# Query sums, two more key tiles and the keys' high part: three transfers in place of engine work, in a fused attention and two-layer kernel

## The chip, the cores and the metric

The kernel runs on one core of one Trainium2 chip. A core has five engines that run side by side: TensorE (PE, with its weight loads as PEld), VectorE (DVE), ScalarE (ACT), GpSimd (POOL) and SyncE (SP, which here only issues transfers). Each works through its own instructions in the order in which the program puts them. The metric is the time of one execution on the device in microseconds; less is better. Before the change the median of three runs is 679.89 us (678.85 to 679.95).

## The reference

```python
q_pool = q.reshape(B, H, S // 2, 2, D).mean(axis=3)     # B 2, H 8, S 1152, D 64
scores = scale * (q_pool @ k.T)                         # 576 pooled queries, 1152 keys
attn = exp(scores - max) / (sum + 1e-9)
x = (attn @ v), heads side by side                      # 1152 tokens, 512 wide
h = x @ w_in1                                           # 512 to 2048
x = where(h >= 1, h, where(h <= -1, 0, (h + 1)**2 / 4)) @ w_out1
h = x @ w_in2
out = (h * sigmoid(h)) @ w_out2
```

Inputs q, k, v are float32; the weights are float64.

## The kernel before

Matrix products are made exact enough by parts: every operand is split into a high part, rounded to the type float32r, and a low part, the difference. The product of two operands is then two or three products of parts. `ident` and `ident_r` are the identity in float32 and in float32r.

Attention runs head by head, 16 of them. For a head, keys, queries and values are loaded with 128 rows on partitions. **Keys**: ACT copies the loaded tile `kraw` into half 0 of `khl`, rounding it (`hi`, line 446); POOL writes the low part into half 1 (`lo_of`, line 138); PE turns the nine pieces, high and low stacked (line 464), and ACT or DVE moves them to `kk`. **Queries**: POOL adds the two rows of a pair into half 0 of `qs` (line 481); SP copies half 0 to half 1 by a transfer (`twice`, line 488); PE turns the four pieces of `qs` with the float32 identity `ident` (line 496); ACT and DVE make the parts `qm`. **Scores** (line 570): PE multiplies a row tile of 128 queries with the 1152 keys in three banks; DVE moves each bank, negated, to a tile `p` and keeps the row minimum (line 577); ACT takes the exponential in place (line 590). There are eight `p` tiles, so two heads' worth. **Values**: the probabilities have to be turned, nine key tiles of 128 by 512 per head. For key tiles 0 to 3 PE turns the four pieces straight from the `p` tiles with `ident` (line 630). For key tiles 4 to 8 SP first copies the columns from `p` to a float32r tile `pr` (line 597; one tile `pr0` for key tiles 4 and 5, one `pr1` for 6 to 8, list `COPIED`), and PE turns them from there with `ident_r` (line 634). ACT moves a turned tile out of its bank and DVE (`KINDS` "psum": lines 608, 609) or POOL ("pool": lines 614, 138) makes the parts `thl`, and PE multiplies them with the value parts (line 647). Queries 512 to 575 of two heads share one row tile, `pt` (lines 676, 685). Behind the attention run the two layers (lines 158, 203, 205).

What order the instructions stand in is settled when the program is built. Every step is an `op` with a due time, the engine with an assumed occupancy and latency, the steps that it needs, and the buffers that it holds (`Buf`, counted in `room`). `plan_out` walks through them with these assumed numbers and gives each engine its list; the rows of order below are its outcome. On the chip each engine follows its list and waits for what is not there yet.

Of the kernel before, what the change touches and what calls it, by code (L numbers as in the profile page):

```python
# [8 lines left out]
F32 = mybir.dt.float32  # L9
# [9 lines left out]
def fused_kernel(  # L19
# [11 lines left out]
    nc = tc.nc  # L31
# [22 lines left out]
    WARM = 7  # L54
    COPIED = ((4, 2), (6, 3))
    AHEAD = 3.0
# [287 lines left out]
    with ExitStack() as at, ExitStack() as keys, ExitStack() as prep:  # L344
# [15 lines left out]
        khls = several(nat, 2, [P, KC, 2, D], F32R, "khl")  # L360
        qss = several(nat, 2, [P, NM, 2, D], F32, "qs")
        kks = several(qk, 3, [P, KC, P], F32R, "kk")
        qms = [several(qk, 2, [P, NM * P], F32R, f"qm{i}") for i in range(2)]
        qts = [several(qk, 2, [P, 3, QT], F32R, f"qt{i}") for i in range(2)]
        ps_ = several(pp, 2 * NM, [P, S], F32, "p")
        pts = several(pp, 1, [P, S], F32, "pt")
# [8 lines left out]
        tiny = fixed.tile([P, 1], F32, name="tiny")  # L375
        room.update(qraw=2, kraw=2, vraw=1, khl=2, qs=2, kk=3, qm=2, qt=2, qtraw=2, qts=1, p=2 * NM, pt=1, **{f"pr{i}": 1 for i in range(len(COPIED))}, thl=THL, pf=PF, vhl=2)
        room.update(y2=2, rb=2, z=1, b=6, y=2, w=1)
# [31 lines left out]
        def inputs(h):  # L409
# [34 lines left out]
            for part in [slice(3 * g, 3 * g + 3) for g in range(3)] if h == 0 else [slice(0, KC)] * 1:  # L444
                n = (part.stop - part.start) / KC
                hi = lambda part=part: nc.scalar.copy(khls[kb.slot][:, part, 0], kraws[kr.slot][:, part])
                khi.append(op(t1, ("ACT", 0.08 + 0.5 * n, 0.17 + 0.51 * n, hi), [lk], [kr, kb]))
                lo = lambda e, part=part: lambda: lo_of(e, khls[kb.slot][:, part, 1], kraws[kr.slot][:, part], khls[kb.slot][:, part, 0])
                ways = [("POOL", 0.2 + 1.175 * n, 0.25 + 1.18 * n, lo(nc.gpsimd))]
                if not h:  # L450
                    ways.insert(0, ("DVE", 0.1 + 0.6 * n, 0.18 + 0.6 * n, lo(nc.vector)))
                klo.append(op(t1 + 0.01, ways, [khi[-1]], [kr, kb], both=not h))
            if h:
# [20 lines left out]

            qb, bank, mb = Buf("qs"), Buf("b"), Buf("qm")
            qm[h] = mb

            def split_q(e):
                t = qraws[qr.slot]
                if h:  # L480
                    e.tensor_add(qss[qb.slot][:, :, 0], t[:, :, 0], t[:, :, 1])
                else:
                    e.tensor_add(qss[qb.slot], *(t[:, :, r].unsqueeze(2).to_broadcast([P, NM, 2, D]) for r in range(2)))

            t3 = base(h - 2) - 0.1 * PERIOD
            if h:
                sq = op(t3, ("POOL", 0.7, 0.76, lambda: split_q(nc.gpsimd)), [lq], [qr, qb])
                twice = lambda: nc.sync.dma_start(out=qss[qb.slot][:, :, 1], in_=qss[qb.slot][:, :, 0])
                sq = op(t3 + 1, ("SP", 0.5, 2.6, twice), [sq], [qb])
            else:  # L490
# [3 lines left out]
            def turn_q():  # L494
                for i in range(NM):
                    nc.tensor.transpose(banks[bank.slot][:, i * P : (i + 1) * P], qss[qb.slot][:, i].rearrange("p a d -> p (a d)"), ident)  # L496

            o = op(t4, ("PE", 0.436, 0.6, turn_q), [sq], [qb, bank])
            o1 = op(t4 + 0.5, ("ACT", 0.483, 0.62, lambda: nc.scalar.mul(qms[mb.slot][0], banks[bank.slot], SCALE)), [o], [bank, mb])

# [117 lines left out]
        def values(h):  # L618
# [5 lines left out]
            for c in range(KC):  # L624
# [12 lines left out]
                if x:  # L637
                    do = lambda x=x[0], f=turn_copy: f(x=x)
                    o = op(tc_, ("PE", 0.27, 0.45, do), [o_r[h, x[0], i] for i in range(NM)], [bank, pr_of[h, x[0]]])
                else:  # L640
# [314 lines left out]
```

## Time and profile before

| | |
|---|---|
| median of three runs | 679.89 us |
| the profiled execution | 680.63 us, its span 678.5 us |
| PE busy, share of the span | 670.0 us, 99% |
| POOL, ACT, DVE busy | 438.0, 420.2, 524.0 us |
| attention, roughly | the first 280 us of the span |
| share of the 16 DMA engines, 20 to 255 us | 0.53 |

A row of the list of groups or of the view by stretches gives busy time; busy PE time contains overlap of one matmul with the next, so what a block of matmuls costs is read from when the next block starts. A row of the waits names who ended an engine's idle time. The chain of work that ended last tells which work set the end.

### The profile page before, as it was taken

Reading aid. Unit: us, or ns where it says so; the run is one execution under the profiler, and the core shown is the slowest. Engines: PE = TensorE matmul, PEld = TensorE weight load, DVE = VectorE, ACT = ScalarE, POOL = GpSimd, SP = SyncE. Lnnn points to the kernel's source line nnn. Section 1 sums busy time; section 2 is a strip of 40 time slices with the busy share of each in tenths; the row PEclk is TensorE's granted clock in tenths of the full one; section 3 lists DMA queues with packets and bytes.
Section 4 is the critical chain, followed back from the end, with each engine's and each line's share of the span. In section 5 each row is a group of like instructions: output and inputs, shape, how many; then the busy total and the mean of one; then the engine's idle time right before and its main releaser. Section 6 shows DMA issues by size and latency. Waiting matters only on the chain.

```text
span 678.5 us, 11815 instructions
## 1 busy us (share of the span) xinstructions
PE 670.0 (99%) x3962; PEld 623.5 (92%) x3962; DVE 524.0 (77%) x1180; ACT 420.2 (62%) x808; POOL 438.0 (65%) x414
## 2 busy tenths in 40 slices
PE   8999999999999999999999999999999999999997
PEld 6899988999999979999999999999999999999996
DVE  6879898988888898389898995996983794892223
ACT  5989998999898888455644443455554543442221
POOL 5788999999797878546646453486853553553221
PEclk8999999999999999999999999999999999999999
DMA  7866655645433356113333231231231331300012
GB/s 214 213 212 177 188 165 169 179 145 173 130 115 109 98 167 205 47 63 109 110 103 117 93 122 34 95 95 61 94 125 37 116 98 38 118 1 0 1 48 93
DMA packets 54988, 75.90 MB, mean 112 GB/s; under 512 B 14736, under 2 KB 40592, under 8 KB 54928
## 3 DMA queue, kind: packets, MB, share of 16 engines
q1 hardware_dynamic: 54640, 74.73, 35.3%
q8 instruction: 31, 0.51, 0.3%
q10 hardware_dynamic: 288, 0.43, 0.2%
q14 instruction: 29, 0.24, 0.1%
HBM read 49.81 MB, written 2.39 MB: 77 GB/s over the span
## 4 chain that ended last, share of the span: by engine, by line
PE 94%; DVE 2%; DMA 2%; ACT 1%; issue 1%; DVEq 0%; ACTq 0%
PE bank L158 30%; PE bank L203 15%; PE bank L205 15%; PE bank L570 12%; PE bank L647 10%; PE bank L630 4%; PE bank L634 3%; PE bank L685 3%; PE bank L464 1%; PE bank L676 1%; DMA pr<-p 1%; PE bank L496 1%; DMA qraw<-in_q_dram 1%; DVE p L577 0%; DVE part L217 0%
## 5 line engine op out<-in xcount | busy, mean ns | idle before, releaser
L138 POOL TENSOR_TENSOR gl<-gf,gh 128x384 fp32r<-128x384 f32 x96 | 110.0, 1147 | 107.3 <-ACT gh L187 104.0
L158 PE MATMUL bank<-xh,whi 128*128 128x384 f32 x384 | 129.7, 338 | 0.0
L158 PE MATMUL bank<-xh,wli 128*128 128x384 f32 x384 | 129.2, 337 | 0.0
L158 PE MATMUL bank<-xl,whi 128*128 128x384 f32 x384 | 129.2, 336 | 0.0
L577 DVE TENSOR_SCALAR_CACHE_REDUCE p<-bank 128x384 f32<-128x384 f32 x192 | 102.0, 551 | 20.7 <-PE bank L570 14.3
L647 PE MATMUL bank<-thl,vhl 128*128 128x512 f32 x288 | 113.4, 429 | 0.0
L138 POOL TENSOR_TENSOR thl<-pf,thl 128x512 fp32r<-128x512 f32 x80 | 103.7, 1298 | 4.0 <-PE bank L647 0.7
L181 DVE TENSOR_TENSOR gf<-bank,gf 128x384 f32<-128x384 f32 x96 | 52.9, 551 | 65.0 <-ACT gf L173 60.6
L570 PE MATMUL bank<-kk,qm 128*128 128x384 f32 x384 | 97.3, 357 | 0.3
L590 ACT ACTIVATE p<-p,low 128x1152 f32<-128x1152 f32 x64 | 81.5, 1274 | 2.7 <-DVE low L587 2.6
L187 ACT CAST gh<-gf 128x384 fp32r<-128x384 f32 x96 | 49.3, 513 | 49.6 <-DVE gf L181 47.6
L158 PEld LDWEIGHTS bank<-xl,whi 128*128 128x128 f32 x384 | 72.1, 188 | 4.2
L158 PEld LDWEIGHTS bank<-xh,whi 128*128 128x128 f32 x384 | 72.1, 188 | 4.0
L138 POOL TENSOR_TENSOR wli<-wf,whi 128x512 fp32r<-128x512 f32 x32 | 43.8, 1369 | 45.6 <-ACT whi L128 45.5
L570 PEld LDWEIGHTS bank<-kk,qm 128*128 128x128 f32 x384 | 66.4, 193 | 7.2 <-DVE thl L609 1.2
L158 PEld LDWEIGHTS bank<-xh,wli 128*128 128x128 f32 x384 | 72.1, 188 | 0.0
L138 POOL TENSOR_TENSOR wlo<-wf,who 128x512 fp32r<-128x512 f32 x32 | 44.0, 1374 | 37.3 <-ACT who L128 37.3
L173 ACT ACTIVATE gf<-bank 128x384 f32<-128x384 f32 x48 | 23.6, 491 | 70.8 <-PE bank L158 64.9
L116 DVE SCALAR_TENSOR_TENSOR wf<-wr,wf 128x512 uint32<-128x512 uint32 x56 | 65.0, 1160 | 1.0
L203 PE MATMUL bank<-gh,wlo 128*128 128x384 f32 x192 | 65.0, 338 | 0.0
L203 PE MATMUL bank<-gh,who 128*128 128x384 f32 x192 | 64.8, 337 | 0.0
L203 PE MATMUL bank<-gl,who 128*128 128x384 f32 x192 | 64.7, 337 | 0.0
(97 smaller groups left out, 1550.8 us busy)
## 6 DMA issues: line engine op xcount, KB each, us to landing
wr<-in_moe_w_in_dram SPq DMA_DIRECT2D x32, 512.0 KB, 3.7
wr<-in_moe_w_out_dram SPq DMA_DIRECT2D x32, 512.0 KB, 3.3
pr<-p SPq DMA_DIRECT2D x64, 192.0 KB, 2.3
pr<-p SPq DMA_DIRECT2D x64, 128.0 KB, 2.2
vraw<-in_v_dram SPq DMA_DIRECT2D x16, 288.0 KB, 3.3
kraw<-in_k_dram SPq DMA_DIRECT2D x15, 288.0 KB, 3.3
qraw<-in_q_dram SPq DMA_DIRECT2D x16, 256.0 KB, 3.4
rb<-row SPq DMA_DIRECT2D x16, 128.0 KB, 3.1
```

The source lines that it names most:

```text
L116: nc.vector.scalar_tensor_tensor(xi, st["top"], 0xC0000000, xi, ALU.bitwise_and, ALU.bitwise_or)
L138: eng.tensor_sub(out, whole, hi.bitcast(F32))
L158: nc.tensor.matmul(ps, lhsT=w[:, c, j * P : (j + 1) * P], rhs=a[:, c, ts_], start=(c == 0 and n == 0), stop=(c == ND - 1 and n == 2),)
L181: nc.vector.tensor_tensor(gf, hps.pop(i), gf, op=ALU.mult if steps[i][0] else ALU.max)
L187: nc.scalar.copy(gh, gf)
L203: nc.tensor.matmul(ps[:, :TB], lhsT=w[:, j, m * P : (m + 1) * P], rhs=a, start=start, stop=stop)
L205: nc.tensor.matmul(ps[:, cols], lhsT=a[:, m * P : (m + 1) * P], rhs=w[:, j, cols], start=start, stop=stop)
L570: nc.tensor.matmul(ps, lhsT=qq[:, c0 : c0 + P], rhs=rhs, start=n == 0, stop=n == last)
L577: nc.vector.tensor_scalar(dst, ps, -1.0, None, ALU.mult, ALU.min, accum_out=mxs[key, t][:, j : j + 1])
L590: nc.scalar.activation(pt(), pt(), AF.Exp, bias=lows[key][:, tt : tt + 1], scale=-1.0, accum_out=sums[key][:, tt : tt + 1])
L630: nc.tensor.transpose(banks[bank.slot][:, i * P : (i + 1) * P], ps_[p_of[h, i].slot][:, c * P : (c + 1) * P], ident)
L647: nc.tensor.matmul(banks[6 + yb.slot], lhsT=lhsT, rhs=thls[tb.slot][i], start=not count, stop=len(count) == 2 * KC - 1)
```

## The change

Three things are done in another way.

- Key tiles 2 and 3 are copied as well: `COPIED` has a third tile, seven of the nine key tiles are turned from copies with `ident_r`, and SP issues twelve copies for a head in place of eight. The `p` tiles become six (`STAGED`).
- The query sums stand once in `qs`, and two transfers on SP put them into both halves of a float32r tile `qd`, from which PE turns them with `ident_r`. For head 0 the sums go to the tile `y2s[0]` and are turned as before.
- For heads 3 to 15 the high part of the keys is not made by ACT. GpSimd issues a second load of the same keys from memory straight into half 0 of `khl`, with a conversion to float32r on the way. The first load stays, for the low part.

The planner's assumed cost of one turn from a copy goes from 0.27 to 0.35 us.

```diff
@@ -52,7 +52,7 @@
     PF = 2
     SLACK = 0.2
     WARM = 7
-    COPIED = ((4, 2), (6, 3))
+    STAGED, COPIED = 6, ((2, 2), (4, 2), (6, 3))
     AHEAD = 3.0
     KINDS = ("psum", "pool", "psum", "pool", "psum", "pool", "psum", "pool", "pool")
     KEVAC = [[("ACT", 0.37, 0.484), ("DVE", 0.476, 0.547)]] * 3
@@ -358,11 +358,12 @@
         kraws = several(nat, 2, [P, KC, D], F32, "kraw")
         vraws = several(nat, 1, [P, KC, D], F32, "vraw")
         khls = several(nat, 2, [P, KC, 2, D], F32R, "khl")
-        qss = several(nat, 2, [P, NM, 2, D], F32, "qs")
+        qss = several(nat, 2, [P, NM, D], F32, "qs")
+        qds = several(nat, 2, [P, NM, 2, D], F32R, "qd")
         kks = several(qk, 3, [P, KC, P], F32R, "kk")
         qms = [several(qk, 2, [P, NM * P], F32R, f"qm{i}") for i in range(2)]
         qts = [several(qk, 2, [P, 3, QT], F32R, f"qt{i}") for i in range(2)]
-        ps_ = several(pp, 2 * NM, [P, S], F32, "p")
+        ps_ = several(pp, STAGED, [P, S], F32, "p")
         pts = several(pp, 1, [P, S], F32, "pt")
 
         prs = [pp.tile([P, NM, n * P], F32R, name=f"pr{i}") for i, (_, n) in enumerate(COPIED)]
@@ -373,7 +374,7 @@
         rbs = several(pp, 2, [P, NM * P], F32, "rb")
         ztail = fixed.tile([P, P], F32, name="ztail")
         tiny = fixed.tile([P, 1], F32, name="tiny")
-        room.update(qraw=2, kraw=2, vraw=1, khl=2, qs=2, kk=3, qm=2, qt=2, qtraw=2, qts=1, p=2 * NM, pt=1, **{f"pr{i}": 1 for i in range(len(COPIED))}, thl=THL, pf=PF, vhl=2)
+        room.update(qraw=2, kraw=2, vraw=1, khl=2, qs=2, qd=2, kk=3, qm=2, qt=2, qtraw=2, qts=1, p=STAGED, pt=1, **{f"pr{i}": 1 for i in range(len(COPIED))}, thl=THL, pf=PF, vhl=2)
         room.update(y2=2, rb=2, z=1, b=6, y=2, w=1)
 
         def clear(what):
@@ -444,12 +445,16 @@
             for part in [slice(3 * g, 3 * g + 3) for g in range(3)] if h == 0 else [slice(0, KC)] * 1:
                 n = (part.stop - part.start) / KC
                 hi = lambda part=part: nc.scalar.copy(khls[kb.slot][:, part, 0], kraws[kr.slot][:, part])
-                khi.append(op(t1, ("ACT", 0.08 + 0.5 * n, 0.17 + 0.51 * n, hi), [lk], [kr, kb]))
+                if h > 2:
+                    cast = lambda: nc.gpsimd.dma_start(out=khls[kb.slot][:, :, 0], in_=k[b, hd].rearrange("(p c) d -> p c d", c=KC))
+                    khi.append(op(t0, ("POOL", 1.0, 4.5, cast), [lq, o_k[h - 2][-1]], [kb]))
+                else:
+                    khi.append(op(t1, ("ACT", 0.08 + 0.5 * n, 0.17 + 0.51 * n, hi), [lk], [kr, kb]))
                 lo = lambda e, part=part: lambda: lo_of(e, khls[kb.slot][:, part, 1], kraws[kr.slot][:, part], khls[kb.slot][:, part, 0])
                 ways = [("POOL", 0.2 + 1.175 * n, 0.25 + 1.18 * n, lo(nc.gpsimd))]
                 if not h:
                     ways.insert(0, ("DVE", 0.1 + 0.6 * n, 0.18 + 0.6 * n, lo(nc.vector)))
-                klo.append(op(t1 + 0.01, ways, [khi[-1]], [kr, kb], both=not h))
+                klo.append(op(t1 + 0.01, ways, [khi[-1], lk], [kr, kb], both=not h))
             if h:
                 khi, klo = khi * 3, klo * 3
             kb2 = kk[h] = Buf("kk")
@@ -472,30 +477,35 @@
                 ways = [(e, occ, lat, (lambda e=e, ev=evac: ev(e)())) for e, occ, lat in KEVAC[g]]
                 o_k[h].append(op(t2 + 0.5, ways, [o], [bank, kb2]))
 
-            qb, bank, mb = Buf("qs"), Buf("b"), Buf("qm")
+            qb, qb2, bank, mb = Buf("qs"), Buf("qd"), Buf("b"), Buf("qm")
+            first_q = y2s[0].rearrange("p (t a d) -> p t a d", a=2, d=D)
             qm[h] = mb
 
             def split_q(e):
                 t = qraws[qr.slot]
                 if h:
-                    e.tensor_add(qss[qb.slot][:, :, 0], t[:, :, 0], t[:, :, 1])
+                    e.tensor_add(qss[qb.slot], t[:, :, 0], t[:, :, 1])
                 else:
-                    e.tensor_add(qss[qb.slot], *(t[:, :, r].unsqueeze(2).to_broadcast([P, NM, 2, D]) for r in range(2)))
+                    e.tensor_add(first_q, *(t[:, :, r].unsqueeze(2).to_broadcast([P, NM, 2, D]) for r in range(2)))
 
             t3 = base(h - 2) - 0.1 * PERIOD
             if h:
                 sq = op(t3, ("POOL", 0.7, 0.76, lambda: split_q(nc.gpsimd)), [lq], [qr, qb])
-                twice = lambda: nc.sync.dma_start(out=qss[qb.slot][:, :, 1], in_=qss[qb.slot][:, :, 0])
-                sq = op(t3 + 1, ("SP", 0.5, 2.6, twice), [sq], [qb])
+                twice = lambda: [nc.sync.dma_start(out=qds[qb2.slot][:, :, x].bitcast(F32), in_=qss[qb.slot]) for x in range(2)]
+                sq = op(t3 + 1, ("SP", 0.9, 3.0, twice), [sq], [qb, qb2])
             else:
                 sq = op(t3, [("DVE", 0.6, 0.69, lambda: split_q(nc.vector)), ("POOL", 1.25, 1.31, lambda: split_q(nc.gpsimd))], [lq], [qr, qb], both=True)
             t4 = base(h - 2) + 0.3 * PERIOD
 
             def turn_q():
                 for i in range(NM):
-                    nc.tensor.transpose(banks[bank.slot][:, i * P : (i + 1) * P], qss[qb.slot][:, i].rearrange("p a d -> p (a d)"), ident)
-
-            o = op(t4, ("PE", 0.436, 0.6, turn_q), [sq], [qb, bank])
+                    to = banks[bank.slot][:, i * P : (i + 1) * P]
+                    if h:
+                        nc.tensor.transpose(to.bitcast(F32R), qds[qb2.slot][:, i].rearrange("p a d -> p (a d)"), ident_r)
+                    else:
+                        nc.tensor.transpose(to, first_q[:, i].rearrange("p a d -> p (a d)"), ident)
+
+            o = op(t4, ("PE", 0.35, 0.53, turn_q) if h else ("PE", 0.436, 0.6, turn_q), [sq], [qb2 if h else qb, bank])
             o1 = op(t4 + 0.5, ("ACT", 0.483, 0.62, lambda: nc.scalar.mul(qms[mb.slot][0], banks[bank.slot], SCALE)), [o], [bank, mb])
 
             def rest():
@@ -636,7 +646,7 @@
                 x = [i for i, (c0, n) in enumerate(COPIED) if c0 <= c < c0 + n]
                 if x:
                     do = lambda x=x[0], f=turn_copy: f(x=x)
-                    o = op(tc_, ("PE", 0.27, 0.45, do), [o_r[h, x[0], i] for i in range(NM)], [bank, pr_of[h, x[0]]])
+                    o = op(tc_, ("PE", 0.35, 0.53, do), [o_r[h, x[0], i] for i in range(NM)], [bank, pr_of[h, x[0]]])
                 else:
                     o = op(tc_, ("PE", 0.436, 0.6, turn), [o_p[h, i] for i in range(NM)], [bank] + [p_of[h, i] for i in range(NM)])
                 parts = split(tc_ + 0.5, bank, NM, [o], tb, KINDS[c])
```

On POOL, in the middle of the attention, before: `khl` from `kraw` is the keys' low part, L614 is the rounded copy of a turned tile, `vhl` the values' low part, `xl` the low part of a finished head pair.

```order
L138 TENSOR_TENSOR vhl_143<-vraw_105,vhl_143 128x9x64
L138 TENSOR_TENSOR thl_139<-pf_140,thl_138 128x512
L138 TENSOR_TENSOR xl<-y_145,xh 128x512
L614 CAST thl_136<-pf_141 128x512
L138 TENSOR_TENSOR khl_106<-kraw_103,khl_106 128x9x64
L138 TENSOR_TENSOR thl_137<-pf_141,thl_136 128x512
L614 CAST thl_132<-pf_140 128x512
L138 TENSOR_TENSOR vhl_143<-vraw_105,vhl_143 128x9x64
```

The same place after. L449 is the new load, L624 the rounded copy of a turned tile.

```order
L624 CAST thl_137<-pf_141 128x512
L449 DMA khl_106<-in_k_dram 128x9x64
L138 TENSOR_TENSOR thl_138<-pf_141,thl_137 128x512
L624 CAST thl_133<-pf_142 128x512
L138 TENSOR_TENSOR vhl_144<-vraw_105,vhl_144 128x9x64
L138 TENSOR_TENSOR thl_134<-pf_142,thl_133 128x512
L138 TENSOR_TENSOR khl_106<-kraw_103,khl_106 128x9x64
L624 CAST thl_139<-pf_141 128x512
```

A load is issued on POOL, and the low part of the keys that waits for its landing stands five rows behind it; both are in the row of instructions that make `thl`.

On SP, while the first two heads are under way, before: `pr` from `p` are copies, `kraw`, `qraw` and `vraw` loads for coming heads.

```order
L597 DMA pr_130<-p_122 128x256
L597 DMA pr_131<-p_122 128x384
L488 DMA qs_109<-qs_109 128x4x64
L424 DMA qraw_98<-in_q_dram 128x4x128
L597 DMA pr_130<-p_123 128x256
L597 DMA pr_131<-p_123 128x384
L420 DMA kraw_103<-in_k_dram 128x576
L597 DMA pr_130<-p_124 128x256
L597 DMA pr_131<-p_124 128x384
```

The same stretch after, up to the load of the same `kraw`:

```order
L607 DMA pr_132<-p_125 128x384
L739 DMA row<-sum 128x4
L607 DMA pr_132<-p_126 128x384
L440 DMA vraw_105<-in_v_dram 128x576
L494 DMA qd_110<-qs_109 128x4x64 x2
L742 DMA rb_147<-row 64x512
L607 DMA pr_130<-p_127 128x256
L607 DMA pr_130<-p_128 128x256
L425 DMA qraw_98<-in_q_dram 128x4x128
L607 DMA pr_130<-p_123 128x256
L421 DMA kraw_103<-in_k_dram 128x576
```

The loads for the coming heads and the doubling of the queries stand behind more copies: this load of keys was row 24 on SP and is row 36.

On PE, the first head's key tiles 2 and 3, before: both are turned from `p` right behind key tiles 0 and 1.

```order
L630 MATMUL bank_70<-ident,p_121 128x128
L630 MATMUL bank_70<-ident,p_122 128x128
L630 MATMUL bank_70<-ident,p_123 128x128
L630 MATMUL bank_70<-ident,p_124 128x128
L630 MATMUL bank_73<-ident,p_121 128x128
L630 MATMUL bank_73<-ident,p_122 128x128
L630 MATMUL bank_73<-ident,p_123 128x128
L630 MATMUL bank_73<-ident,p_124 128x128
L570 MATMUL bank_75<-kk_111,qm_115 128x384
L570 MATMUL bank_75<-kk_111,qm_116 128x384
```

After, with scores of the next head (L580) and the first product with the values (L657) ahead of them:

```order
L657 MATMUL bank_76<-thl_133,vhl_143 128x512
L580 MATMUL bank_73<-kk_113,qm_117 128x384
L580 MATMUL bank_73<-kk_113,qm_118 128x384
L580 MATMUL bank_72<-kk_113,qm_117 128x384
L580 MATMUL bank_72<-kk_113,qm_118 128x384
L644 MATMUL bank_75<-ident_r,pr_130 128x128 x4
L657 MATMUL bank_76<-thl_134,vhl_143 128x512
L657 MATMUL bank_76<-thl_135,vhl_143 128x512
L644 MATMUL bank_74<-ident_r,pr_130 128x128 x4
```

Tiles 2 and 3 of the first head are now turned from the copy `pr_130`, behind the products that stood behind them.

## Rows read from the trace of the kernel before

**Rows 1.** The page: busy times; the chain that ended last, by engine and line.

```profile
PE 670.0 (99%) x3962; PEld 623.5 (92%) x3962; DVE 524.0 (77%) x1180; ACT 420.2 (62%) x808; POOL 438.0 (65%) x414
...
PE bank L158 30%; PE bank L203 15%; PE bank L205 15%; PE bank L570 12%; PE bank L647 10%; PE bank L630 4%; PE bank L634 3%; PE bank L685 3%; PE bank L464 1%; PE bank L676 1%; DMA pr<-p 1%; PE bank L496 1%; DMA qraw<-in_q_dram 1%; DVE p L577 0%; DVE part L217 0%
```

**Rows 2.** Stretches, attention: length; busy times and counts; clock; DMA share; GB/s.

```profile
20.00:255.00 235.00, 233.24 (x1609) 211.41 (x1610) 203.59 (x662) 213.95 (x416) 205.94 (x208) 1.00 0.53 160
```

**Rows 3.** Timeline of PE, one engine: start, us, line, what, count.

```profile
126.41 0.46 PE L634 MATMUL bank<-ident_r,pr 128*128 128x128 f32 x4
126.70 0.46 PE L647 MATMUL bank<-thl,vhl 128*128 128x512 f32 x1
127.00 0.86 PE L570 MATMUL bank<-kk,qt 128*128 128x384 f32 x4
...
133.47 0.60 PE L496 MATMUL bank<-ident,qs 128*128 128x128 f32 x4
133.83 0.48 PE L647 MATMUL bank<-thl,vhl 128*128 128x512 f32 x1
134.15 0.51 PE L570 MATMUL bank<-kk,qm 128*128 128x384 f32 x2
134.50 0.60 PE L630 MATMUL bank<-ident,p 128*128 128x128 f32 x4
134.85 0.48 PE L647 MATMUL bank<-thl,vhl 128*128 128x512 f32 x1
135.17 0.37 PE L464 MATMUL bank<-ident_r,khl 128*128 128x128 f32 x3
```

**Rows 4.** Groups, whole span: the two turns of probabilities; the rounding on ACT.

```profile
L630 PE MATMUL bank<-ident,p 128*128 128x128 f32 x256 | 37.2, 273 | 0.3 <-DVE p L577 0.3
L634 PE MATMUL bank<-ident_r,pr 128*128 128x128 f32 x320 | 37.0, 239 | 0.7 <-DVE wf L120 0.6
L446 ACT CAST khl<-kraw 128x576 fp32r<-128x576 f32 x15 | 10.3, 689 | 1.9 <-POOL khl L138 1.0 <-PE bank L464 0.6 <-DMA vraw<-in_v_dram 0.3
```

**Rows 5.** Groups on POOL, 20 to 255 us: busy, mean ns, idle before and releasers.

```profile
L614 POOL CAST thl<-pf 128x512 fp32r<-128x512 f32 x72 | 44.4, 618 | 13.6 <-ACT pf L613 10.3 <-PE bank L634 3.2
L138 POOL TENSOR_TENSOR khl<-kraw,khl 128x576 fp32r<-128x576 f32 x12 | 17.3, 1442 | 0.4 <-ACT khl L446 0.2 <-PE bank L647 0.2
L481 POOL TENSOR_TENSOR qs<-qraw 128x256 f32<-128x256 f32 x12 | 8.9, 738 | 7.0 <-PE bank L496 6.4 <-DMA pr<-p 0.6
```

**Rows 6.** Timeline of SP: start, us, line, what is issued, count.

```profile
14.11 2.54 SPq L597 DMA_DIRECT2D pr<-p  x4
16.74 0.62 SPq L488 DMA_DIRECT2D qs<-qs  x1
17.41 0.66 SPq L424 DMA_DIRECT2D qraw<-in_q_dram  x1
18.16 1.16 SPq L597 DMA_DIRECT2D pr<-p  x2
19.37 0.59 SPq L420 DMA_DIRECT2D kraw<-in_k_dram  x1
```

**Rows 7.** Issues of transfers: KB of one, median us from issue to landing.

```profile
pr<-p SPq DMA_DIRECT2D x64, 128.0 KB, 2.2
kraw<-in_k_dram SPq DMA_DIRECT2D x15, 288.0 KB, 3.3
qs<-qs SPq DMA_DIRECT2D x15, 128.0 KB, 3.1
```

**Rows 8.** Stretches of ten us: the third from the start.

```profile
20.00:30.00 10.00, 10.00 (x66) 8.55 (x67) 9.32 (x32) 9.82 (x20) 7.03 (x9) 1.00 0.92 229
```

**Rows 9.** Chain of waits, 20 to 255 us: share by line; pieces (start, us, what).

```profile
by line: PE bank L570 31.2%; PE bank L647 25.2%; PE bank L630 9.8%; PE bank L634 8.9%; PE bank L685 6.4%; PE bank L464 3.3%; PE bank L676 2.9%; DMA pr<-p 2.7%; PE bank L496 2.2%; issue 1.2%; DVE p L577 1.1%; DVE thl L609 0.8%; DVE bank L108
...
80.67 2.95 DMA pr<-p
...
240.94 3.35 DMA pr<-p
```

## Prediction

> **What bounds the kernel now.** I read the page first. PE is busy for 99% of the span, and the chain that ended last lies on PE nearly throughout [rows 1]: what the change is worth is PE time saved, less the time in which PE is made to wait. The change lies in the attention, so I read one stretch of it, 20 to 255 us. There PE is busy for 233.24 of 235 us at granted clock 1.00, which is the level of 2.4 GHz; ACT is busy for 213.95 us, POOL for 205.94, DVE for 203.59 [rows 2]. PE is the bound, but three engines stand at 87% to 91%, and each feeds it. The reader should see both: every microsecond off PE counts, and little room is left to move work to the others. Third, busy PE time contains overlap, so I read the cost of a turn from the starts of blocks in the timeline [rows 3]. The groups on POOL, SP's timeline and the transfers came last, since that is where the change puts work.
>
> **Part 1: cheaper turns on PE.** A block of four turns from `p` starts at 134.50, the product behind it at 134.85 and the next block at 135.17: 0.67 us for block and product. With a block of turns from a copy the same pair runs from 126.41 to 127.00, 0.59 us [rows 3]. The difference is 0.08 us for four. Two more key tiles in 16 heads are 32 blocks: 32 x 0.08 = 2.6 us. The query turns: block and product run from 133.47 to 134.15, 0.68 us [rows 3], so a query block with `ident_r` should save 0.68 - 0.59 = 0.09, but its neighbours differ; I use 0.07 to 0.09. Fifteen heads (head 0 stays) make 1.0 to 1.4, say 1.1. The sum is 3.7 us. Another view gives the upper end: the groups' mean busy time per turn is 37.2 us / 256 = 145 ns from `p` and 37.0 / 320 = 116 ns from copies [rows 4], 29 ns apart, and 128 + 60 turns x 29 ns = 5.5 us; that busy time is modelled, so I take the starts' 3.7. Nothing hides PE's work, so these 3.7 us would all come off the time if no wait takes their place.
>
> **Part 2: ACT loses work.** Thirteen roundings of 0.689 us [rows 4] go: 9.0 us of ACT, some 8 of them within the stretch, which takes ACT from 91% to about 88%. None of it is on the chain. What it can give back is on POOL: POOL's rounded copies wait 10.3 us for ACT [rows 5].
>
> **Part 3: POOL gets thirteen loads to issue.** No row shows a transfer issued by POOL. From below: SP issues a load of the same keys in 0.59 us [rows 6]. From above: POOL's own work on the same keys takes 1.44 us [rows 5]; far above lies 3.3 us, the median from issue to landing of such a load on SP [rows 7], if POOL were held until the data are there. The issue writes addresses and moves no data, so it is nearer to the first two; between them I take 1.0 us. That is 13 us. POOL's idle time in the stretch is 235 - 205.94 = 29.1 us, less 3.7 because the stretch shortens: 25.4. Of it 10.3 are waits for ACT, which part 2 shortens, and 6.4 are sums that wait for PE to have turned the older queries out of `qs` [rows 5]; now a transfer empties `qs`, so these go. The two make 16.7 us that can be filled. At 1.0 us the loads fit, POOL rises to about (205.9 + 13) / 231.3 = 95%, and they cost nothing directly. Queued behind the load on POOL are the parts `thl` that PE's products wait for; the load itself waits for PE to have turned the keys of two heads before. The low part of the keys stands five rows behind the load. Between them the order has a rounded copy, 0.62 us, and three differences of at most 1.44 us each [rows 5], under 4.9 us; a load that lands 3.3 us [rows 7] behind its issue is there in time, one that needs over 4.9 us stops POOL.
>
> The Trainium skill (DMA: Bandwidth & Descriptors, SWDGE vs HWDGE vs iDMA) speaks against the change: the descriptors of a load issued by GpSimd are computed by code on GpSimd's own cores, where those of SP's loads come from hardware. Its section Latency and other measured facts gives about 1 us to the first byte; by that figure, as an estimate, thirteen loads take 13 us, the same sum as mine. No run here shows it yet.
>
> **Part 4: SP and the transfers.** SP issues 64 more copies at 0.58 us each (two in 1.16) and 15 more doublings at 0.62 [rows 6]: 37 + 9 = 46 us, 3 us a head, of about 15. In steady state SP has that room. Early on it has not: from 14.11 us on it issues without a gap [rows 6]. There the order puts the keys' load, at 19.37 before, twelve rows later; at 0.6 us that is 7 us, about 26.6, and with 3.3 us of landing [rows 7] the data are there at 30. The first head's tiles 2 and 3 now need a landed copy, 2.2 us [rows 7] behind its issue, where PE had turned them at once. The order puts other products in between, so I take 0.5 us of waiting here, between 0 and the 2.2 of one landing. The traffic: 64 x 128 KB, 15 x 128 KB and 13 x 288 KB are 14 MB in 235 us, 60 GB/s on top of 160 at a share of 0.53 [rows 2]; in proportion 0.73. In the third ten us the share is 0.92 already [rows 8]. Chains through a copy exist before: two pieces of 2.95 and 3.35 us, 2.7% of the stretch in all [rows 9]; under more traffic such pieces grow. PE's waits in the stretch were 235 - 233.24 = 1.8 us [rows 2]. With POOL at 95% and six `p` tiles in place of eight I let them grow by 0.7 us, bounded by 0 and by a doubling, and by a gain of the same 1.8 if ACT's relief removes them.
>
> **The sum.** -3.7 (PE) + 0.5 (early copies) + 0.7 (more waits) = -2.5 us. The profiled execution takes 680.63 us for a span of 678.5; against it the sum gives 678.1. The median of the runs is 679.89, 0.7 below the profiled one; since the sum is a difference, I set it against the median: 677.4 us.
>
> **Rivals.** *POOL becomes the bound (slower).* The place is POOL's queue between 20 and 230 us, the price is the issue of one load. If only the 16.7 us can be filled, it decides from (16.7 + 3.7) / 13 = 1.6 us for one load; with POOL packed without a gap, from 29.1 / 13 = 2.2 us. At 1.8 us the loads take 23.4, 6.7 more than can be filled, and the time is 679.9 - 3.7 + 6.7 = 682.9; at 2.2 it is 688. For it: POOL is at 88%, and the load converts and writes runs of 64 elements where SP's copies write long rows. Against it: SP's 0.59 us.
>
> *The transfers take the gain back (no change).* Each copy's landing grows with the share of the DMA engines; if a head meets 0.15 us more of a wait for copies, through `pr` or through the six `p` tiles, 16 heads cost 2.4 us, on top of my 1.2: 679.9 - 3.7 + 3.6 = 679.8. For it: the chain's pieces through copies [rows 9], the third ten us [rows 8]. Against it: after 40 us SP and the engines have room.
>
> *Everything is hidden and ACT's relief removes waits too (faster).* -3.7 - 1.8 = 674.4, or the 5.5 of the upper end: the same.
>
> *The change does less than it says.* If the query block's 0.09 is its neighbours' doing, part 1 is 2.6 and the time 678.5, at the edge of my own case.
>
> **How the numbers follow.** My forecast, 675.6 to 678.5, gets 0.48; no change, 678.5 to 681.3, 0.27; POOL or its landings as the bound, above 681.3, 0.20; everything hidden, below 675.6, 0.05. About 0.2%, 1.4 us, is what a measurement of this kernel can tell from no change, so faster is 0.53, same 0.27, slower 0.20. The range reaches from 675.2 to 683.0: it leaves out about 0.04 below and 0.12 above, where a load's issue costs over 1.8 us.
>
> **What would show it.** In the profile after: turns of queries and of key tiles 2 and 3 spaced as those from copies (block and product 0.59 us); 13 roundings of keys gone from ACT; POOL's busy time, or its idle time before the loads, up by 13 us and the waits of L481 for PE gone; PE's busy share in 20 to 250 us still near 99%. I am wrong if one load takes over 1.6 us on POOL, if POOL waits for the second load's landing, or if PE waits for copies in most heads.

## The result and the profile after

The changed kernel takes 688.02 us (median of 4 runs, 686.28 to 689.47) against 679.84: a ratio of 1.0125, 95% interval 1.0108 to 1.0141. It is 8.2 us slower, where 677.4 was forecast and 683.0 was the upper end of the range. The profiled execution of after is its fastest run, 686.28 us with a span of 684.2; against the span of 678.5 before it shows 5.7 of the 8.2 us.

The page after: busy times, packets, and the chain that ended last, as [rows 1].

```profile
PE 669.0 (98%) x3962; PEld 618.8 (90%) x3962; DVE 519.5 (76%) x1176; ACT 415.6 (61%) x799; POOL 449.3 (66%) x427
...
DMA packets 87310, 90.11 MB, mean 132 GB/s; under 512 B 38864, under 2 KB 72912, under 8 KB 87248
...
PE bank L158 30%; PE bank L203 15%; PE bank L205 15%; PE bank L580 8%; PE bank L657 8%; DMA pr<-p 5%; PE bank L644 4%; PE bank L695 2%; DVE p L587 2%; PE bank L640 1%; PE bank L686 1%; PE bank L469 1%; DMA wr<-in_moe_w_in_dram 1%; DMA qraw<-in_q_dram 1%; DVE kk L474 0%
```

PE does the same 3962 instructions in 669.0 us, only 1.0 less than before; its idle time, span less busy, goes from 8.5 to 15.2 us. Copies `pr<-p` hold 5% of the chain, 1% before. The same stretch as [rows 2]:

```profile
20.00:255.00 235.00, 227.70 (x1574) 203.89 (x1572) 195.59 (x638) 204.16 (x398) 213.93 (x217) 1.00 0.82 214
```

PE completes 1574 instructions there, 35 fewer than before, and is idle for 7.3 us (1.8 before). The DMA share is 0.82 (0.53), the clock 1.00. What PE waited for in this stretch (total us, times, longest), before and then after:

```profile
PE bank L634 <- DVE wf L120: 0.6, 1, 0.6
PE bank L570 <- DVE thl L609: 0.5, 1, 0.5
PE bank L630 <- DVE p L577: 0.3, 1, 0.3
```

```profile
PE bank L644 <- DMA pr<-p: 3.6, 6, 1.3
PE bank L640 <- DVE p L587: 1.4, 1, 1.4
PE bank L657 <- POOL thl L624: 0.8, 1, 0.8
PE bank L657 <- POOL thl L138: 0.5, 1, 0.5
PE bank L580 <- DVE thl L619: 0.4, 1, 0.4
```

No wait for a copy is listed before; after, six of them make 3.6 us, half of PE's idle time there. The groups on POOL, as [rows 5], and the median landings in the stretch, as [rows 7]:

```profile
L624 POOL CAST thl<-pf 128x512 fp32r<-128x512 f32 x71 | 43.1, 611 | 12.0 <-ACT pf L623 8.3 <-PE bank L644 3.5
L138 POOL TENSOR_TENSOR khl<-kraw,khl 128x576 fp32r<-128x576 f32 x13 | 18.5, 1424 | 4.6 <-DMA khl<-in_k_dram 3.7 <-PE bank L657 0.9
L449 POOL DMA_DIRECT2D khl<-in_k_dram x12 | 12.4, 1031 | 0.0
L487 POOL TENSOR_TENSOR qs<-qraw 128x256 f32<-128x256 f32 x12 | 8.8, 734 | 0.2 <-DMA kraw<-in_k_dram 0.2
```

```profile
pr<-p SPq DMA_DIRECT2D x115, 128.0 KB, 3.3
pr<-p SPq DMA_DIRECT2D x58, 192.0 KB, 3.4
kraw<-in_k_dram SPq DMA_DIRECT2D x12, 288.0 KB, 4.1
khl<-in_k_dram POOLq DMA_DIRECT2D x12, 288.0 KB, 5.8
```

The new load holds POOL for 1.03 us and lands 5.8 us after its issue, and the small copies land after 3.3 us in place of 2.2. POOL waits for it before four of the keys' low parts, 3.7 us in all. The longest of these waits on POOL's timeline (start, us, wait in brackets):

```profile
44.19 1.02 POOL L449 DMA_DIRECT2D khl<-in_k_dram  x1
45.21 0.63 POOL L624 CAST thl<-pf 128x512 fp32r<-128x512 f32 x1
45.79 0.75 POOL L487 TENSOR_TENSOR qs<-qraw 128x256 f32<-128x256 f32 x1
46.49 1.29 POOL L138 TENSOR_TENSOR thl<-pf,thl 128x512 fp32r<-128x512 f32 x1
47.86 0.61 POOL L624 CAST thl<-pf 128x512 fp32r<-128x512 f32 x1
48.55 1.30 POOL L138 TENSOR_TENSOR thl<-pf,thl 128x512 fp32r<-128x512 f32 x1
51.56 1.43 POOL L138 TENSOR_TENSOR khl<-kraw,khl 128x576 fp32r<-128x576 f32 x1 [1.71 <-DMA khl<-in_k_dram]
52.94 1.17 POOL L624 CAST thl<-pf 128x512 fp32r<-128x512 f32 x2
```

The low part stands six rows behind the load, 5.7 us; the load needs some 7.3, POOL stands for 1.71 us, and the parts for PE's products are queued behind. In the same microseconds the chain runs through two copies, one after the other (start, us, what):

```profile
45.16 6.75 DMA pr<-p
...
51.98 3.27 DMA pr<-p
```

### The profile page after: what moved, and what is told of

Same layout as the page of the kernel before. It is cut to its first block, busy times and chain, and to the rows that moved or that the text cites. A ratio compares the mean times of both kernels' runs of the same rounds, so it can differ in the third digit from the quotient of the medians.

```text
span 684.2 us, 12077 instructions
## 1 busy us (share of the span) xinstructions
PE 669.0 (98%) x3962; PEld 618.8 (90%) x3962; DVE 519.5 (76%) x1176; ACT 415.6 (61%) x799; POOL 449.3 (66%) x427
## 2 busy tenths in 40 slices
DMA packets 87310, 90.11 MB, mean 132 GB/s; under 512 B 38864, under 2 KB 72912, under 8 KB 87248
## 4 chain that ended last, share of the span: by engine, by line
PE 85%; DMA 6%; DVE 4%; ACT 2%; issue 1%; POOL 0%; DVEq 0%; SPq 0%; ACTq 0%; POOLq 0%
PE bank L158 30%; PE bank L203 15%; PE bank L205 15%; PE bank L580 8%; PE bank L657 8%; DMA pr<-p 5%; PE bank L644 4%; PE bank L695 2%; DVE p L587 2%; PE bank L640 1%; PE bank L686 1%; PE bank L469 1%; DMA wr<-in_moe_w_in_dram 1%; DMA qraw<-in_q_dram 1%; DVE kk L474 0%
## 5 line engine op out<-in xcount | busy, mean ns | idle before, releaser
L657 PE MATMUL bank<-thl,vhl 128*128 128x512 f32 x288 | 114.7, 431 | 1.7 <-POOL thl L624 1.2
L580 PE MATMUL bank<-kk,qm 128*128 128x384 f32 x384 | 96.2, 351 | 1.5 <-DVE p L587 0.5
L580 PEld LDWEIGHTS bank<-kk,qm 128*128 128x128 f32 x384 | 65.7, 189 | 9.8 <-DVE thl L619 1.8
L619 DVE TENSOR_TENSOR thl<-bank,thl 128x512 fp32r<-128x512 f32 (+1 forms) x88 | 56.3, 649 | 12.9 <-ACT thl L618 11.1
```

The source lines that it names most:

```text
L580: nc.tensor.matmul(ps, lhsT=qq[:, c0 : c0 + P], rhs=rhs, start=n == 0, stop=n == last)
L619: o2 = op(target + 0.3, ("DVE", 0.6 * f, 0.683 * f, lambda: nc.vector.tensor_sub(tl(), ps(), th().bitcast(F32))), [o1], [bank, tb])
L657: nc.tensor.matmul(banks[6 + yb.slot], lhsT=lhsT, rhs=thls[tb.slot][i], start=not count, stop=len(count) == 2 * KC - 1)
```

## The experiments

Times are medians. The kernel before took 680.3 to 680.8 us beside them, and the ratios are to it.

**Each edit alone.** From the kernel before, one part of the diff at a time. e2 has only the second load of the keys; e3 only the copies:

```diff
+    STAGED, COPIED = 6, ((2, 2), (4, 2), (6, 3))
+        ps_ = several(pp, STAGED, [P, S], F32, "p")
```

e4 and e8 have only the query sums, through `qd`, with two groups of copies; e4 has room for one tile `qs`, e8 for two (seven `p` tiles).

> The kernel before with the casting load for heads 3 to 15 alone. Theory A: 31 us more per transfer engine, share about 0.66, copies land in about 2.6 us in place of 2.2, 681 us. Theory B: no loss, 678 to 680 us. Theory C: POOL rises by 13 us of issue and some 4 us of waiting, 682 to 684 us.

> The kernel before with three copied groups and six p tiles alone. 32 blocks of turns are cheaper on PE, worth 2.6 us. Theory A: 27 us more per transfer engine, share about 0.65, 678 to 680 us. Theory B: 684 us or more. Theory C: 677 us.

> The kernel before with the two transfers for the queries and their cheaper turns alone (one qs tile in place of two, for room). All theories: 10 us more per transfer engine, 1.1 us less on PE, 678 to 680 us; a loss of over 1 us would speak for something that none of them names.

> The kernel before with the queries' two transfers alone, as e4_queries_alone, but with the two qs tiles of the change and seven p tiles in place of eight, for room. If the loss of e4_queries_alone came from its single qs tile: 679 to 680 us. Theory D, with sums that wait for transfers and those for the turns of older queries: 682 to 685 us.

Measured: e2 680.06 (0.9993, 0.9983 to 1.0002), e3 680.74 (1.0007, 0.9995 to 1.0019), e8 680.84 (1.0008, 0.9999 to 1.0018), e4 684.65 (1.0061, 1.0043 to 1.0080). No edit alone moves the time; e4's loss is that of its single tile `qs`, in which POOL's next sum waits for the transfers (5.3 us). So no edit alone gains its share of the forecast 3.7 us either, and the loss comes from combinations. In e2 POOL already waits 2.4 us for the load, and no time is lost by it:

```profile
L138 POOL TENSOR_TENSOR khl<-kraw,khl 128x576 fp32r<-128x576 f32 x13 | 18.5, 1425 | 2.4 <-DMA khl<-in_k_dram 2.4
```

**Pairs.** e1 is the changed kernel with ACT rounding the keys; e7 has the queries as before; e9 has the two groups of copies as before:

```diff
-                if h > 2:                                              (e1)
+                if h > NH:
```

```diff
-    STAGED, COPIED = 6, ((2, 2), (4, 2), (6, 3))                       (e9)
+    STAGED, COPIED = 7, ((4, 2), (6, 3))
```

> The changed kernel with the keys' high part made by ACT again; seven copied tiles, six p tiles and the doubled query transfers stay. Theory A (the 16 transfer engines are overloaded, so copies land late): of the 69 us that the change adds to each engine the load is 31, so the share from 20 to 255 us falls from 0.82 to about 0.69, a copy lands in about 2.7 us in place of 3.3, and most of the 8 us come back: about 681 us. Theory B (six p tiles and three single pr tiles make the chain through copies too tight, whatever the load): stays at 685 us or more. Theory C (POOL, with 13 issues of 1.03 us and waits for landings, is what PE waits for): 676 to 678 us.

> The changed kernel with the queries as before: one transfer from half to half, turned with the float32 identity. Copies and casting load stay. Theory D: the sums wait for PE's turns alone, 679 to 681 us. Theory A: 10 of the 69 us per transfer engine go, share about 0.77, still 684 to 686 us.

> The two other edits without the copies: the converting load of the keys and the query sums that are doubled by two transfers into a tile of their own, with two groups of copied key tiles as before. It completes the set of pairs: copies with the load gave 686.43, copies with the sums 686.42, and each edit alone between 680.1 and 680.8. If every pair overloads the transfer engines or the plan (any two edits are too many): 685 to 687 us. If the copies are needed for the loss, because p tiles and copies are what waits when a transfer lands late: 680 to 682 us, the engines' share in 20 to 255 us about 0.73 and the landing of the copies for pr under 3.0 us.

Measured: e1 686.42 (1.0108, 1.0073 to 1.0144), e7 686.43 (1.0099, 1.0077 to 1.0120), e9 681.84 (1.0020, 1.0011 to 1.0029). The copies are in both pairs that lose over 5 us; the pair without them loses 1.2 us, little but beyond its interval. The two large losses do not look alike. In e7 the DMA share is 0.79 and POOL waits 5.9 us for the load. In e1 the share is only 0.67; there the chain passes through the query transfers:

```profile
137.95 4.31 DMA qd<-qs
...
142.43 0.10 POOL qs L487
...
143.12 1.27 POOL thl L138
144.39 0.04 issue
144.43 0.50 PE bank L657
```

POOL's next sum cannot write `qs` until an older sum has left it by transfer; the part `thl` stands behind that sum, and PE's product behind that. This is one place: over the stretch POOL's sums wait 6.0 us in e1 and 7.0 before the change [rows 5], so that their waiting by itself is not what e1 loses.

**Traffic, issue or waiting?** e5 is the changed kernel, with its order, and a load of one key tile in nine; the other eight high parts are not renewed, so its scores are not those of the reference. e12 to e14 are e3 with something added that nobody waits for: the same load into an unused tile (e12), the same with whole rows (e13), and a fill of about 1.03 us on POOL (e14):

```diff
+                    extra = lambda: nc.gpsimd.dma_start(out=dms[0][:, :, 0], in_=k[b, hd]...)   (e12)
+                    op(t0, ("POOL", 1.0, 4.5, extra), [lq, o_k[h - 2][-1]], [Buf("dm")])
```

> The changed kernel in its own order, instruction for instruction, but the casting load moves one of the nine pieces of the keys (32 KB in place of 288); the other eight pieces keep older high parts, so the scores are not those of the reference. Theory A (the transfer engines are overloaded): the load's 31 us per engine fall to about 4, the share from 0.82 to about 0.71, copies land in 2.7 us, 682 to 684 us. Theory D (the query sums on POOL wait for transfers that wait for PE, and POOL's parts come late): nothing changes in that, 686 to 688 us. Theory C (POOL's issues): no change either, if an issue stays near 1.03 us.

> The kernel with the copies alone (680.74 us), ACT rounding the keys as before, and in 13 heads one more load beside it: the same converting load with rows of 64 elements, issued by GpSimd at the same place, into a tile that nobody reads (its data are left unused). Only the traffic and the issue are added, and nobody waits for it. If the traffic (or the issue) is what the copies cannot bear: 685 to 687 us, as with the load in use (686.43). If it is the waiting of GpSimd's low part for the load's landing: 680.5 to 682 us.

> As the run before, but the unused load writes whole rows of 576 elements: the same bytes and the same conversion in an eighth to a ninth of the packets. If the transfer engines pay for packets: share in 20 to 255 us about 0.10 lower than with narrow rows, 681 to 683 us. If they pay for bytes, or for the conversion of each element: the same time as with narrow rows. The issue on GpSimd gets cheaper too (0.5 to 0.6 us), which the next run tells apart.

> The kernel with the copies alone, and in place of the unused load a fill of an unused tile on GpSimd of about 1.03 us at the same place in 13 heads: GpSimd's time without any traffic. If GpSimd's time is what costs: 684 to 687 us. If the transfers are: 680.5 to 682 us.

Measured: e5 681.93 (1.0032, 1.0017 to 1.0047), e12 682.07 (1.0031, 1.0016 to 1.0045), e13 683.35 (1.0031, 1.0014 to 1.0048), e14 681.02 (1.0000, 0.9991 to 1.0009). The stretch 20 to 255 us of e12, e13 and e14, one after the other:

```profile
20.00:255.00 235.00, 231.13 (x1599) 208.74 (x1599) 199.27 (x655) 216.02 (x420) 215.58 (x219) 1.00 0.79 208
```

```profile
20.00:255.00 235.00, 230.36 (x1592) 208.53 (x1591) 196.77 (x649) 213.92 (x416) 208.59 (x217) 0.99 0.71 207
```

```profile
20.00:255.00 235.00, 231.96 (x1604) 208.98 (x1605) 199.58 (x656) 216.34 (x420) 215.81 (x220) 1.00 0.64 193
```

POOL's time is free: with 215.81 us of work the time is that of before. The traffic is nearly free: e12 has the share of e7, 0.79, and costs 1.3 us over e3, where e7 costs 5.7. Nor are later landings of the copies enough: in e12 they land after 3.4 and 4.0 us (128 and 192 KB), no earlier than in the changed kernel. So some 4 us of e7's loss appear only when the load is in use; that is POOL's wait for it or the order that goes with it, since in e7 ACT's rounding is gone and the planned order is another. e5 agrees: with the order in place but a load that lands after 3.8 us, the low part waits 0.0 us for it and the loss is 1.6 us. But e5 takes traffic away too (share 0.69, the copies of 128 KB land after 2.9 us), so it does not tell the two apart. (e5's issue is also shorter, 0.58 us; by e14 that is worth nothing.) Whole rows take the share from 0.79 to 0.71 and the landing from 5.9 to 3.9 us, but not the time.

**Can the order be mended?** The planner assumes 4.5 us for the load and about 3.1 for a copy; 5.8 and 3.3 were measured. e15 tells it the one, e16 the other, e6 both; e17 is e6 with three tiles `qs`, e10 is e1 with three, e18 is e7 with seven `p` tiles, and e19 has one more copied key tile in place of two, and seven `p` tiles.

```diff
-                    khi.append(op(t0, ("POOL", 1.0, 4.5, cast), ...        (e15, e6, e17)
+                    khi.append(op(t0, ("POOL", 1.0, 6.5, cast), ...
-                o_r[...] = op(..., ("SP", 0.2 + 0.18 * n, 2.7 + 0.2 * n, copy), ...   (e16, e6, e17)
+                o_r[...] = op(..., ("SP", 0.2 + 0.18 * n, 3.7 + 0.2 * n, copy), ...
```

> The changed kernel, planned with the landings that its trace shows: 6.5 us in place of 4.5 for the casting load, one more for a copy (4.1 in place of 3.1 for two tiles). The work is the same, the order another. Theory A with the engines truly full: 686 us or more, whatever the order. If the order, made for transfers that land earlier, is what costs: 681 to 684 us.

> The changed kernel, with one number of the planner changed: the converting load is planned with 6.5 us to its landing in place of 4.5 (measured 5.7). The same work and traffic; only the order moves, the low part of the keys above all. With both landings told (this one and 1 us more for the copies) the kernel took 684.12. If GpSimd's wait for this load is the part that the order can mend: 684 to 685.5 us, and the low part's wait for the load (3.7 us) is gone. If it is PE's waits for copies: still 687 to 689 us.

> The other half: the copies for pr are planned with 1 us more to their landing, the load as in the changed kernel. If PE's waits for copies (3.6 us in the changed kernel) are what the order can mend: 684 to 685.5 us and these waits under 1.5 us. If it is GpSimd's wait for the load: still 687 to 689 us.

> The changed kernel with both landings told and three tiles qs: every wait that was found is taken care of, and the traffic stays (share about 0.82). If the waits were all of the loss, PE's cheaper turns show: 679 to 681 us. If the traffic itself costs (the unused load cost 1.4 us beside the copies alone): 682 to 684 us.

> Copies and query sums without the converting load (686.42 us), with three tiles qs in place of two, so that GpSimd's sum for the next head does not wait until the transfers of an older sum have left its tile. If that wait on GpSimd is what copies and sums together cost: 681 to 683 us, and PE's waits for GpSimd's parts (4.0 us of 6.1) fall under 2. If it is the load on the transfers or the order as a whole: 685 to 687 us.

> The kernel with copies and converting load and the queries as before (686.43 us), with seven tiles p in place of six (the space that the queries' second tile took is free there). If six p tiles leave the planned order too little room, so that late landings and small moves of the order turn into waits of PE: 681 to 683 us. If it is the transfers' load or the order apart from p: 685 to 687 us.

> The changed kernel with one more copied key tile in place of two (tile 3 alone), which pays for a seventh tile p: half of the added copies, all of the load and of the query sums. If six p tiles are the cause: 681 to 683 us. If the loss goes with the added copies' traffic: about half of the step from the kernel without added copies (681.84) to the changed one (688.02), 684 to 686 us. If it is the order as such: anything up to 691 us.

| kernel | median us | ratio, interval | PE idle in 20 to 255 us | mean granted clock of its runs |
|---|---|---|---|---|
| the changed kernel | 688.02 | 1.0125 (1.0108 to 1.0141) | 7.3 | 1.000 |
| e6, both told | 684.12 | 1.0068 (1.0045 to 1.0091) | 3.0 | 0.997 to 1.000 |
| e15, load told | 691.43 | 1.0159 (1.0143 to 1.0176) | 9.0 | 0.994 to 0.997 |
| e16, copies told | 691.45 | 1.0159 (1.0144 to 1.0174) | 4.6 | 0.990 to 0.994 |
| e17, both told, three `qs` | 684.80 | 1.0069 (1.0054 to 1.0084) | 5.2 | 0.999 to 1.000 |
| e10, e1 with three `qs` | 685.60 | 1.0081 (1.0064 to 1.0098) | 5.2 | 0.995 to 1.000 |
| e18, e7 with seven `p` | 688.66 | 1.0124 (1.0091 to 1.0156) | 5.2 | 0.988 to 0.996 |
| e19, one tile less | 690.09 | 1.0146 (1.0126 to 1.0166) | 5.0 | 0.996 to 0.998 |

Both told, the low part waits 0.0 us for the load and PE 0.7 us for copies in place of 3.6, and the time falls by 3.9 us. Each half by itself shortens its own wait: in e15 the low part waits 2.2 us for the load in place of 3.7, in e16 PE waits 0.4 us for copies in place of 3.6. The other wait grows, to 4.5 us for copies in e15 and 4.4 for the load in e16:

```profile
L138 POOL TENSOR_TENSOR khl<-kraw,khl 128x576 fp32r<-128x576 f32 x13 | 18.6, 1428 | 2.2 <-DMA khl<-in_k_dram 2.2
```

```profile
PE bank L644 <- DMA pr<-p: 0.4, 1, 0.4
```

But the time of each is some 3 us *longer* than the changed kernel's: the theory that a mended wait comes off the time falls. e15, e16, e6 and the changed kernel do the same work with the same traffic, and lie between 684.1 and 691.5 us by their order alone. Two more theories fall: too few `p` tiles (e18, e19) and, for the most part, the tile `qs` (e10, whose interval overlaps e1's). What e15 and e16 lose over the changed kernel can for the most part be put down to PE's clock. PE's busy time over the span, for the same instructions, in e15 and e16:

```profile
PE 672.2 (98%) x3962; PEld 623.4 (90%) x3962; DVE 523.0 (76%) x1171; ACT 417.7 (61%) x804; POOL 450.4 (65%) x427
```

```profile
PE 674.2 (98%) x3962; PEld 624.1 (91%) x3962; DVE 518.2 (75%) x1172; ACT 417.6 (61%) x803; POOL 449.1 (65%) x427
```

That is 3.2 and 5.2 us more than the 669.0 of the changed kernel, while PE's idle time, span less busy, is 16.8 and 13.8 us against 15.2: e16's order waits less and still takes longer. In e16 PE waited 2.05 us for POOL, until 121.35, and then (stretches of 2 us; the figure before the DMA share is the granted clock):

```profile
118.00:120.00 2.00, 0.86 (x7) 0.54 (x5) 2.00 (x8) 0.85 (x2) 1.34 (x1) 1.00 0.70 240
120.00:122.00 2.00, 0.65 (x2) 0.56 (x3) 0.73 (x2) 0.68 (x2) 1.92 (x4) 0.72 0.48 119
122.00:124.00 2.00, 2.00 (x13) 1.82 (x12) 0.82 (x2) 1.11 (x3) 1.92 (x3) 0.50 0.35 127
124.00:126.00 2.00, 2.00 (x7) 1.60 (x8) 1.21 (x3) 1.94 (x5) 1.92 (x3) 0.50 0.42 116
126.00:128.00 2.00, 2.00 (x12) 1.80 (x11) 1.37 (x4) 1.17 (x3) 1.81 (x2) 0.57 0.80 191
128.00:130.00 2.00, 2.00 (x14) 1.84 (x14) 1.81 (x6) 1.03 (x2) 2.00 (x2) 1.00 0.34 106
```

PE runs at the level of 1.2 GHz for some 6 us, about 3 us of work lost, more than the wait itself. The same fall stands twice in e15 and once in e1, e10 and e13, each time right behind one wait of 1.8 to 2.2 us; once more in e16, at 260 us, behind four waits of 0.2 to 0.5 us; and once each in e18 and e19, at 256 and 258 us, behind two and three waits of 0.4 to 0.6 us. The profiled execution of after, whose longest wait in the stretch is 1.4 us, has none. Added up over such stretches from 14 us on, two microseconds times the missing part of the clock, the falls are worth 3.4 us in e15 and 5.1 in e16, an estimate near PE's extra busy time. (Busy time moves with the order too: e17, without a fall, has 671.5 us.) In e18 the four runs go the same way: 687.37 us at a mean clock of 0.996, 688.22 at 0.994, 689.10 at 0.990, 692.66 at 0.988.

## Why the prediction was wrong

**Part 1, cheaper turns: right by the block, somewhat too large in the sum.** From PE's timeline of after:

```profile
134.22 0.60 PE L640 MATMUL bank<-ident,p 128*128 128x128 f32 x4
134.57 0.48 PE L657 MATMUL bank<-thl,vhl 128*128 128x512 f32 x1
134.89 0.37 PE L469 MATMUL bank<-ident_r,khl 128*128 128x128 f32 x3
...
136.87 0.45 PE L504 MATMUL bank<-ident_r,qd 128*128 128x128 f32 x4
137.16 0.93 PE L657 MATMUL bank<-thl,vhl 128*128 128x512 f32 x3
...
138.27 0.45 PE L644 MATMUL bank<-ident_r,pr 128*128 128x128 f32 x4
138.56 0.47 PE L657 MATMUL bank<-thl,vhl 128*128 128x512 f32 x1
138.87 0.37 PE L469 MATMUL bank<-ident_r,khl 128*128 128x128 f32 x3
```

A block from `p` with its product takes 0.67 us, one from a copy 0.60, and a query block now lasts 0.29 until the next start, 0.36 in [rows 3]. Taken from start to start over 14 to 290 us, turns with a wait behind them left out, a turn from `p` took 94 ns before, a query's 98 before and 76 after; but a turn from a copy went from 76 to 79. So the gain is 128 x 15 + 60 x 22 ns less 320 x 3 ns, 2.3 us in place of 3.7.

**Part 2, ACT: right and idle.** ACT's busy time fell in the stretch from 213.95 to 204.16 us, and POOL's wait for ACT only from 10.3 to 8.3.

**Part 3, POOL: the price right, the landing wrong.** The issue took 1.03 us against the assumed 1.0, POOL's busy share in the stretch came to 91%, not 95%, and the sum's waits of L481 went as forecast (0.2 us left). The rival of POOL as the bound did not come about, and e14 shows that 13 us more on POOL cost nothing; that this rival gives 688 us at 2.2 us for an issue meets the measured time by chance. What failed is the landing of 3.3 us that the load was given: that was the landing of SP's load at a DMA share of 0.53. The converting load landed after 5.8, past the limit of 4.9 us that the prediction itself named (its terms, 0.62 + 3 x 1.44, make 4.94), and POOL waited 3.7 us for it, one of the prediction's own signs of being wrong. The Trainium skill (DMA: Bandwidth & Descriptors, Specifications) asks for at least 512 B in a transfer for the full rate. For the engines e12 against e13 agrees with it: the load in rows of 256 B against the same bytes in whole rows, share 0.79 to 0.71, landing 5.9 to 3.9 us; the kernel's time did not follow. The page of after shows 38864 packets under 512 B, 14736 before.

**Part 4, the transfers: the step that failed.** The share was worked out by bytes, 0.73; it came to 0.82. The keys' load, forecast 7 us later at 26.6, was issued at 29.5 us, but no wait of PE is put down to it. More important, the waits were mis-sized. They stand in the sum with 0.5 us for early copies and 0.7 for the rest of the stretch, at most 1.8; PE's idle time there grew by 5.5 us. Of these, 1.9 are early copies, the waits for `pr<-p` between 14 and 46 us, and 1.7 later ones for copies; the others are waits for DVE and POOL. The rival "the transfers take the gain back" named the right place, copies and their landing, with too small a price (0.15 us a head; 5.5 us over 16 heads are 0.34), and no case held that the planned order, made for earlier landings, would by itself move the time.

**The sum.** Of the span's 5.7 us, idle time of PE is +6.7 and busy time -1.0. Turns account for -2.3 of the latter, and some 1.3 us went into other instructions: the turns of the shared tile `pt` took 92 ns in place of 82, 0.7 us for 72 of them, and the rest is open. Before's own span holds two stretches of 2 us, from 8 us on, at granted clock 0.65 and 0.50 that after's does not, so the pair of profiles may show the loss too small, by an estimate of at most 1.7 us (4 us less what these clocks grant).

**Shown and open.** Shown: the loss is not the price of an issue (e14), not the traffic or later copies by themselves (e12), not the rows' width (e13), not 2.4 us of POOL's waiting for the load by themselves (e2), not the `p` tiles (e18). It needs the added copies (without them, e9, 1.2 us are lost), and with them the load (e7) or the query sums (e1). The same work costs 3.8 to 11.1 us over before, by the planned order, and some of the spread is PE's clock. Not shown: by what way copies and load lose together. That late landings stop POOL and that the parts for PE stand behind it fits the traces, and the time fell when both landings were told (e6), but each wait mended by itself gave nothing back. Open too: what copies and query sums lose by, since a third tile `qs` changed little (e10), and when a wait is followed by a fall of the clock. No order was found in which the cheaper turns come through, and no kernel here beats the one before beyond its interval.

## What to carry to other kernels

A transfer added to a chain is priced by its landing under the traffic of the new kernel, with its rows' width and its conversion, not by the landing of the nearest transfer before; then one looks at what stands behind the waiting instruction on its in-order engine. Where a planner sets the order from assumed times, a change of work is also a change of order: here the order alone was worth 7 us, more than the 2 us that the change saves on PE, so several orders of the new work have to be measured before the edit is judged. Beside idle time one reads the busy time of the bound engine and its clock: e16 waits less than the changed kernel and takes longer. Edits that cost nothing alone have to be measured together.

## What the runs showed of the hardware

A load that GpSimd issues costs it 1.03 us with 1152 rows of 64 elements and 0.58 us with 128 such rows (e5), and lands after 4.7 to 6.0 us beside the traffic of these runs (medians), 3.9 with whole rows (e13). Behind a wait of PE of 2.05 us its granted clock was at half for some 6 us in e16, so that this wait cost over twice its length; behind three waits of 0.4 to 0.5 us, one soon after the other, it fell in e19 as well. A wait of 2.7 us in e4 was not followed by such a fall, and what decides is open. The same 288 KB by a converting load kept the DMA engines busier in rows of 256 B than in whole rows (share 0.79 against 0.71), and landed later (5.9 us against 3.9).
